# Last copies of a sequence on VectorE behind a subtraction, and a new order of the last units, in an attention and expert-routing kernel

## Chip, cores, metric

One core of a Trainium2 chip runs the whole program. The metric is device time of one execution in microseconds (us). The kernel before takes 702.86 us, the median of three runs (702.64 to 704.63).

## What is computed

Inputs are q, k, v of shape (8 sequences, 8 heads, 576 tokens, 64) and the weights of a mixture of 8 experts.

```
out_up    = repeat(softmax(0.125 q_d k_d^T) v_d, 4)        # q_d, k_d, v_d: means over groups of 4 tokens
out_local = softmax(where(|i-j| < 4, 0.125 q k^T, -1e9)) v
x         = (out_up + out_local) as 4608 tokens x 512
logits    = x @ w_gate                                     # 4608 x 8
# all (token, expert) pairs by falling logit; an expert takes 576 tokens at most
out[mask_e] = relu(x[mask_e] @ w1[e]) @ w2[e]
```

The order of the logits decides which expert a token goes to, so the logits of all tokens must stand before the first expert can be chosen.

## The kernel before, in words

The program has two stages. The attention stage (class Attention) makes x and the logits, the expert stage counts logits against thresholds, picks an expert, gathers its 576 tokens and runs its two products. This document is about the attention stage; the expert stage's code is untouched.

Attention works on 36 units of 128 tokens. A unit is four windows of 32 tokens of local attention: `loc_s` (s0, s1: local scores into PSUM, then row maximum L544 and subtraction L545 on VectorE, and an exponential L547 on ScalarE, called four pieces later), `loc_t` (t: transposes L555 of the exponentials, copied out of PSUM by ScalarE, L566), `loc_v` (v0, v1: product with v L577, and `norm`, three VectorE instructions L453, L454, L456 for each half), `log_a` (adds the up part, L587; on VectorE for units below 27 and for unit 35, on GpSimd for 27 to 34), `store` (x to DRAM on SyncE's queue), `log_t` (lt: four transposes of x L597 and a copy by ScalarE) and `log_m` (lm: the logits, copied to `lg` by VectorE). For a unit below UF = 33 the copy of lt is an fp16 high part (`hi`, L609, ScalarE) and an fp16 remainder (`lo`, L610, VectorE), and lm is eight short fp16 products (L625, L628). For units 33, 34 and 35 lt is one fp32 copy (L604, ScalarE) and lm is four fp32 products (L621).

Each of the 8 sequences b also needs: eight transposes of q and k (`trw`, L330), called here by letter, half and side: q00, k00, q01, k01, q10, k10, q11, k11; after each, two copies of 64x512 out of PSUM by `evac` (L310 to L316). One transpose of the 16 last groups (`trt`, L343) with two copies of 128x256. Sums over four tokens on GpSimd (`gsum`, L303, L306, called after k01 and k11, and `gsum_v` after k11). The down-sampled attention (`down_s`: scores, maximum L370, subtraction L372, exponentials L378; `down_t`: transposes L394, L399 and a copy each by `evac`; `down_v`: products and norm).

`evac` picks the engine of a copy: it counts calls (a pair counts once) and takes VectorE where the pattern EV has a 1. EV = (0, 0, 0, 0, 1) over 13 calls of a sequence moves from place to place. PSUM buffers called g are a ring of six (NG), shared by trw, trt, t, v0, v1, lt, lm and the down products: a product waits until the buffer six uses back has been read.

The order is written out: `run` gives every stage of every unit a due time, sorts by it, and emits the instructions in that order; each engine and each DMA queue executes its own in that order. The due time of a stage is u + LOC, and for LOC of 2 and more it is u + 2 + (LOC - 2) * (1 - 0.14 * max(u - 33, 0)) + max(0.72 - 0.55 u, 0). So v0 and v1 of unit 35 are due at 36.842 and 36.843, `add` (`log_a`) of units 32, 33 and 34 at 36.425, 37.425 and 38.085, lt of units 32 to 35 at 37.433, 38.433, 38.952 and 39.472, and lm of units 31 to 35 at 39.317, 40.317, 41.317, 41.433 and 41.548. `after(n, f)` puts a call n pieces (TensorE stages) later. `setup` (class Routing) turns logits into sort keys in steps; units 0 to 24 are done early (L725 to L728), its comparisons L834 at 38.45 and later, and units 25 to 35 right after the last logits.

Of the kernel before, what the change touches and what calls it, by code (L numbers as in the profile page):

```python
# [11 lines left out]
AF = mybir.ActivationFunctionType  # L12
OP = mybir.AluOpType
# [13 lines left out]
GM = 128  # L27
# [3 lines left out]
NT = NTOK // 128  # L31
E, F = 8, 1024
XS = 32.0
# [13 lines left out]
FH = 2  # L47
FL = 4
FT = 3
PEL = ("s0", "s1", "t", "v0", "v1", "lt", "lm")  # L50
TW = (0.23, 2.44)
DW = (0.15, 1.9)
# [9 lines left out]
XB = 6  # L62
NPT = 2
PEV = (0,0)
EV = (0, 0, 0, 0, 1)
UPB = 6
UPE = 1.5
VWE, VWU = 2.0, 33
CMP = (7, 38.1, 0.05)
ADDU = UPB * 9 // 2  # L70
DX = 0
SETUP = {24: 0, 35: 25}
SPACE = 0.365
GS = 32.0
# [8 lines left out]
E1 = 0.55  # L83
UE = 33
CE = 0.14
UF = 33
UL = 30
TX = 0.0
VX = 0.0
# [15 lines left out]
class Attention:  # L105
# [88 lines left out]
    def after(self, n, f, key=None):  # L194

        self.due.append((self.now + n, f, key))
# [112 lines left out]
    def evac(self, out, in_, more=False):  # L309

        self.nev += not more
        ev = EV if self.nev > EN0 else EV0
        if ev[self.nev % len(ev)]:
# [9 lines left out]
    def trw(self, b, which, hh, s):  # L323

        nc = self.nc
        src = self.nat[which, b]
        p = self.ps.tile([128, 2, GM, 2], F32, name="g", bufs=NG)
        for a in range(2):
            for fp in range(2):
                nc.tensor.transpose(p[:, a, :, fp], src[:, 4 * hh + 2 * a + s, 2 * fp:2 * fp + 2].rearrange("p f d -> p (f d)"),  # L330
                                    self.ident)
        t = self.dest(b, which)[64 * s:64 * s + 64, 2 * hh:2 * hh + 2]
        for par in range(2):
            self.evac(t[:, :, par:4 * GM:2], p[64 * par:64 * par + 64].rearrange("p a i f -> p a (i f)"), par)

    def trt(self, b):

# [230 lines left out]
    def loc_v(self, u, g):  # L568
        nc = self.nc
        if g == 0:  # L570
            self.x[u] = self.wk.tile([128, HD], F32, name="x", bufs=XB)
        x = self.x[u]
        o = self.ps.tile([128, 512], F32, name="g", bufs=NG)
        pt = self.ptw[u % NPT]
        for h in range(4):
            for i in range(2):
                nc.tensor.matmul(o[64 * i:64 * i + 64, 65 * h:65 * h + 65],  # L577
                                 pt[:, 2 * (h % 2) + i, 2 * g + h // 2].rearrange("p b q -> p (b q)"),
                                 self.vw[u % 4][:, i, 4 * g + h], start=True, stop=True)
        self.norm(o, x[:, 256 * g:256 * g + 256].rearrange("p (h d) -> p h d", h=4), 4, 1.0)  # L580
        if g and u == NT - 1:
            self.log_a(u)

    def log_a(self, u):
        nc = self.nc
        x = self.x[u]
        (nc.gpsimd if ADDU <= u < NT - 1 else nc.vector).tensor_tensor(x, x, self.up[u], op=OP.add)  # L587

    def store(self, u):
        getattr(self.nc, STQ).dma_start(self.x_dram[128 * u:128 * u + 128], self.x[u])  # L590
# [1 line left out]
    def log_t(self, u):  # L592
        nc = self.nc
        x = self.x[u]
        p = self.ps.tile([128, 4, 128], F32, name="g", bufs=NG)
        for c in range(4):
            nc.tensor.transpose(p[:, c], x[:, 128 * c:128 * c + 128], self.ident)  # L597
        pf = p.rearrange("p c t -> p (c t)")
        if u >= UF:
            if u < NT - 1:  # L600
                xt = self.wk.tile([128, HP, G], F32, name="kdt").rearrange("p h k -> p (h k)")[:, :512]
            else:
                xt = self.wk.tile([128, H, D], F32, name="xu", bufs=1).rearrange("p h d -> p (h d)")
            nc.scalar.activation(xt, pf, AF.Copy, scale=XS * GS)  # L604
            self.xt[u] = xt.rearrange("p (c t) -> p c t", c=4)
            return
        xt = self.wk.tile([128, 2, 4, 128], F16, name="xt", bufs=TB)
        hi = xt[:, 0].rearrange("p c t -> p (c t)")
        nc.scalar.activation(hi, pf, AF.Copy, scale=XS)  # L609
        self.after(FT if u < UE - 2 else 1, lambda: nc.vector.scalar_tensor_tensor(xt[:, 1].rearrange("p c t -> p (c t)"), pf, XS, hi,  # L610
                                                              op0=OP.mult, op1=OP.subtract), ("x", u))
        self.xt[u] = xt

    def log_m(self, u):
# [3 lines left out]
        l = self.ps.tile([128, 2, E], F32, name="g", bufs=NG)  # L618
        if u >= UF:
            for c in range(4):  # L620
# [12 lines left out]
    def transposes(self, b):  # L633
        out = []
        for hh in range(2):
            for s in range(2):
                for w in "qk":
                    def f(w=w, hh=hh, s=s):
                        self.trw(b, w, hh, s)
                        if b and s and w == "k":  # L640
                            self.gsum(b, "k", 2 * hh)
                            self.gsum(b, "q", 2 * hh)
                            if hh:
                                self.gsum_v(b)

                    out.append(f)

        return out[:2] + [lambda: self.trt(b)] + out[2:]
# [5 lines left out]
    def run(self, after, ready):  # L654
# [14 lines left out]
        for b in range(B):  # L669
            u0, up = 9 * b // 2, 9 * (b - 1) // 2  # L670
            t = self.transposes(b)
# [13 lines left out]
            if b + 1 < B:  # L685
                for i, (w, at) in enumerate(NEXT):
                    at = max(up + at + (SH1 if b == 1 else 0), -1.0) if b else LD1[i]
                    f = lambda b=b, w=w: self.load_nat(b + 1, w[0], int(w[1]) if w[1:] else None)
# [15 lines left out]
        work = [(at, 0, i, f, False) for i, (at, f) in enumerate(other)]  # L704
        work += [(at, 1, i, f, True) for i, (at, _, f) in enumerate(fill)]
        work += [(at, 1, 10 ** 6 + i, f, False) for i, (at, f) in enumerate(loads)]
        for u in range(NT):
            if u > 1:
                for c in range(4):
                    at = max(u - (VWT0 if u < UV else VWE if u >= VWU else VWT) + VWS * c, u - 3.999 + LOC["v0"])  # L710
                    f = lambda u=u, c=c: self.load_vw(u, (c,))
                    work.append((at, 0, 0, (lambda f=f: self.paced(f)) if at > PACE0 else f, False))
            for j, (name, lag) in enumerate(LOC.items()):
                at = u + lag
                if lag >= 2.0:

                    at = u + 2.0 + (lag - 2.0) * (1.0 - CE * max(u - UE, 0)) + max(E0 - u * E1, 0.0)
                if u >= UL:
                    at += {"t": TX, "v": VX, "v0": VX, "v1": VX}.get(name, 0.0)
                if name == "add" and u == NT - 1:  # L720
                    continue
                if name == "up":
                    at = max(at - (UPE if u >= NT - 2 else 0.0), end[(4 * u + 3) // NW])
                work.append((at, 2, j, stage[name](u), name in PEL))
                if name == "lm" and u in SETUP:  # L725
                    steps = after(SETUP[u], u + 1)
                    work += [(at + SPACE * k if u == NT - 1 or k < CMP[0] else CMP[1] + CMP[2] * k, 3, k,
                              lambda g=steps: next(g, None), False) for k in range(24)]  # L728
        work.sort(key=lambda z: z[:3])
        for *_, f, pe in work:  # L730
# [45 lines left out]
class Routing:  # L776
# [86 lines left out]
    def next(self, mm):  # L863
        if self.pad:
            self.behind_(mm, self.pad)
        return mm
# [637 lines left out]
```

## Time and profile before

| | us |
|---|---|
| median of three runs | 702.86 |
| the profiled execution, its own time | 703.13 |
| its span, first to last instruction | 701.5 |
| around the span | 1.63 |
| last logits of unit 35 copied (L622) at | 252.2 |
| TensorE / VectorE / ScalarE / GpSimd busy in the span | 648.6 / 521.7 / 337.7 / 245.9 |

Times in rows are microseconds from the start of the span. PE is TensorE's products, PEld its weight loads, DVE VectorE, ACT ScalarE, POOL GpSimd, SP SyncE. A row of the timeline gives start, length, engine, line, operation, output and inputs, count; in brackets is how long the engine sat idle before it and what ended that. Lengths of neighbours on one engine overlap a little; the step from start to start is the price.

### The profile page before, as it was taken

How to read it: one execution, taken by the hardware profiler on the slowest of the kernel's cores; microseconds unless marked ns; L12 is line 12 of the kernel's file. 1: busy time of each engine (PE TensorE's matmuls, PEld its weight loads, DVE VectorE, ACT ScalarE, POOL GpSimd, SP SyncE). 2: the span in 40 equal slices, each digit the busy share in tenths (PEclk: the TensorE clock that was granted, in tenths of full speed). 3: DMA queues.
4: the chain of work that ended last, by engine and by line, in shares of the span. 5: the costliest groups of instructions: out<-in, count | busy, mean ns of one | idle time of the engine just before them, and what ended most of it. 6: DMA issues, size and time to landing. Idle time of an engine off the chain costs nothing.

```text
span 701.5 us, 21944 instructions
## 1 busy us (share of the span) xinstructions
PE 648.6 (92%) x8938; PEld 451.3 (64%) x8938; DVE 521.7 (74%) x1544; ACT 337.7 (48%) x650; POOL 245.9 (35%) x320
## 2 busy tenths in 40 slices
PE   7789999899898957999999999999999999999994
PEld 4577777778787744764674575674674764755741
DVE  5697879878789887988887797897897876624500
ACT  4568778788686513523432443444334424424410
POOL 4886485665927412203303204104104115202011
PEclk9899999999999975999999999999999999999997
DMA  9967878868786614507308627548358169714001
GB/s 264 237 166 222 233 188 235 240 184 223 200 221 171 209 68 139 170 1 262 114 6 311 129 93 243 110 155 213 76 213 203 29 244 211 296 39 97 1 30 39
DMA packets 132157, 113.73 MB, mean 162 GB/s; under 512 B 81240, under 2 KB 109912, under 8 KB 132056
## 3 DMA queue, kind: packets, MB, share of 16 engines
q1 hardware_dynamic: 124760, 90.76, 45.7%
q0 software_dynamic: 6432, 20.98, 9.5%
q8 instruction: 71, 1.16, 0.7%
q10 hardware_dynamic: 864, 0.58, 0.3%
q14 instruction: 30, 0.25, 0.1%
HBM read 85.74 MB, written 19.46 MB: 150 GB/s over the span
## 4 chain that ended last, share of the span: by engine, by line
PE 50%; DVE 17%; issue 16%; ACT 7%; DMA 4%; POOL 4%; SPq 1%; ACTq 0%; POOLq 0%; DVEq 0%
PE pX L1332 16%; PE pH L1291 14%; PE g L577 2%; PE pR L886 2%; PE g L555 2%; DVE wl L1214 2%; PE s L535 2%; PE g L330 2%; POOL out_dram L1342 1%; PE g L597 1%; DMA nat<-in_k_dram 1%; PE pH L1198 1%; ACT kt L316 1%; POOL xg L1229 1%; ACT qt L316 1%
## 5 line engine op out<-in xcount | busy, mean ns | idle before, releaser
L1291 PE MATMUL pH<-xt,wh 128*128 128x256 f16 (+1 forms) x1024 | 191.2, 286 | 1.2 <-ACT xt L1250 0.5
L1332 PE MATMUL pX<-wh,ht 128*128 128x512 f16 (+1 forms) x640 | 178.0, 379 | 0.0
L1291 PE MATMUL pH<-xt,wl 128*128 128x320 f16 (+1 forms) x512 | 144.6, 286 | 0.0
L1332 PEld LDWEIGHTS <-ht 128*128 128x128 f16 (+1 forms) x960 | 82.7, 100 | 94.7 <-issue 4.7
L1332 PE MATMUL pX<-wl,ht 128*128 128x512 f16 (+1 forms) x320 | 117.6, 379 | 0.0
L1291 PEld LDWEIGHTS <-wh 128*128 128x128 f16 x1024 | 97.6, 98 | 29.6 <-issue 5.3
L1342 POOL DMA_INDIRECT out_dram<-y,idx x40 | 42.3, 1058 | 178.3 <-ACT y L1339 156.1
L1315 ACT ACTIVATE ht<-pH 128x512 f16<-128x512 f32 (+1 forms) x128 | 45.6, 407 | 114.4 <-PE pH L1291 114.4
L1214 DVE SCALAR_TENSOR_TENSOR wl<-nat,wh 128x512 f16<-128x512 f32 x128 | 83.5, 686 | 16.1 <-ACT wh L1212 13.7
L1339 ACT ACTIVATE y<-pX 128x512 f32<-128x512 f32 (+1 forms) x40 | 23.7, 594 | 101.4 <-PE pX L1332 58.9
L1318 DVE SCALAR_TENSOR_TENSOR ht<-pH,ht 128x512 f16<-128x512 f32 (+1 forms) x128 | 52.3, 449 | 26.1 <-ACT ht L1315 25.6
L1212 ACT ACTIVATE wh<-nat 128x1024 f16<-128x1024 f32 x64 | 67.3, 1053 | 3.8 <-DMA nat<-in_moe_w_dram 3.8
L1229 POOL DMA_INDIRECT xg<-x_dram,idx x40 | 43.1, 1079 | 61.6 <-DVE used L1112 33.4
L1291 PEld LDWEIGHTS <-wl 128*128 128x128 f16 x512 | 49.9, 98 | 12.7 <-issue 0.8
L566 ACT COPY pt<-g 64x512 f32<-64x512 f32 x72 | 41.8, 580 | 27.5 <-PE g L555 26.5
L577 PE MATMUL g<-vw,pt 128*64 128x65 f32 x1152 | 43.5, 225 | 4.0 <-issue 1.5
L577 PEld LDWEIGHTS g<-vw,pt 128*64 128x64 f32 x1152 | 37.8, 137 | 10.5 <-issue 5.0
L330 PE MATMUL g<-ident,nat 128*128 128x128 f32 x256 | 40.4, 283 | 4.2 <-DMA nat<-in_q_dram 3.7
L1031 POOL MEMSET f<- 128x1 bf16 x8 | 0.8, 106 | 118.3 <-DVE sumf L940 44.1
L1258 DVE SCALAR_TENSOR_TENSOR xs<-xg,xs 128x512 f16<-128x512 f32 (+1 forms) x30 | 20.4, 688 | 28.3 <-ACT xs L1257 28.1
L316 ACT COPY kt<-g 64x512 f32<-64x512 f32 (+1 forms) x60 | 38.3, 638 | 6.5 <-PE g L330 5.5
L303 POOL TENSOR_TENSOR gtmp<-kt 128x576 f32<-128x576 f32 x14 | 16.1, 1147 | 54.7 <-ACT kt L316 39.4
(229 smaller groups left out, 1155.5 us busy)
## 6 DMA issues: line engine op xcount, KB each, us to landing
nat<-in_moe_w_dram SPq DMA_DIRECT2D x28, 1024.0 KB
vw<-in_v_dram SPq DMA_DIRECT2D x136, 78.0 KB
x_dram<-x SPq DMA_DIRECT2D x36, 256.0 KB
nat<-in_q_dram SPq DMA_DIRECT2D x32, 256.0 KB
nat<-in_k_dram SPq DMA_DIRECT2D x32, 256.0 KB
nat<-in_v_dram SPq DMA_DIRECT2D x28, 256.0 KB
up<-up_dram SPq DMA_DIRECT2D x9, 256.0 KB
nat<-in_moe_w_dram SPq DMA_DIRECT2D x4, 512.0 KB
```

What stands on the lines that cost most here:

```text
L316: self.nc.scalar.copy(out, in_)
L330: nc.tensor.transpose(p[:, a, :, fp], src[:, 4 * hh + 2 * a + s, 2 * fp:2 * fp + 2].rearrange("p f d -> p (f d)"), self.ident)
L566: self.nc.scalar.copy(out, in_)
L577: nc.tensor.matmul(o[64 * i:64 * i + 64, 65 * h:65 * h + 65], pt[:, 2 * (h % 2) + i, 2 * g + h // 2].rearrange("p b q -> p (b q)"), self.v ...
L1212: nc.scalar.activation(hi, r, AF.Copy, scale=sc)
L1214: nc.vector.scalar_tensor_tensor(lo[:, a:a + LOP], r[:, a:a + LOP], sc, hi[:, a:a + LOP], op0=OP.mult, op1=OP.subtract)
L1229: self.fetched = nc.gpsimd.indirect_dma_start(out=xg[:n], out_offset=None, in_=self.x, in_offset=bass.IndirectOffsetOnAxis(ap=idx[:n, c:c ...
L1291: mm = nc.tensor.matmul(p[:, s, :s1 - s0], w[d][a][:, 128 * f:128 * f + 128], xt[:, b, d, s0:s1], start=j == 0, stop=j == len(seq) - 1)
L1315: last = nc.scalar.activation(hi, q, AF.Relu)
L1318: low = nc.vector.scalar_tensor_tensor(lo, q, 0.0, hi, op0=OP.max, op1=OP.subtract)
L1332: mm = nc.tensor.matmul(p[o:o + m], ht[:, f, h0:h0 + m], w[4 + f // 2][b][:, 512 * (f % 2):512 * (f % 2) + 512], start=j < parts, stop=j > ...
L1342: i = nc.gpsimd.indirect_dma_start(out=self.out, in_=y[:n], in_offset=None, out_offset=bass.IndirectOffsetOnAxis(ap=idx[:n, c:c + 1], axis=0))
```

## The change

In sequences 2 to 7 the two copies of k11 always go to VectorE, and they are emitted four pieces after the transpose with the sums that follow (`after(FK, ...)`), which is behind the subtraction L545 of the unit then running. These copies no longer count in `evac`, so a sequence has 12 counted calls, and the new EV, a pattern of six, hits the same two places each time: `trt` and k01. From sequence 2 on this gives:

- to VectorE: trt of 2, 3, 4, 6, 7, k01 of 2, 4, 5, 6, 7, k11 of 2, 3, 4, 6, 7 (k11 of 5 was there and moves behind the subtraction);
- to ScalarE: q11 of 2, q00, q01, k10 of 4, q10 of 6, k00 and q11 of 7, and five copies of transposed probabilities (`down_t`); in `down_t` of 7 the two last copies change places.

Among the last units: unit 33 takes the fp16 way (UF = 34); the remainder of unit 31 is put behind the norms of unit 35; the fp32 copies of lt are made in halves; the add of unit 35 is split, its first 256 columns on GpSimd in `loc_v` (due 36.842) and its second on VectorE (36.843); lt of 35 moves to 39.0, ahead of lm of 31, lm of 34 to 39.5, ahead of lm of 32 and 33, lm of 35 to 41.4; of the early comparisons the first moves to 35.34, the second to 39.1.

```diff
+FK = 4
-EV = (0, 0, 0, 0, 1)
+EV = (0, 1, 0, 0, 0, 0)
+ENDS = {("lt", 35): 39.0, ("lm", 34): 39.5, ("lm", 35): 41.4}
-CMP = (7, 38.1, 0.05)
+CMP = (7, 35.34, 39.1)
-UF = 33
+UF = 34
@@ trw
-        for par in range(2):
-            self.evac(t[:, :, par:4 * GM:2], p[64 * par:64 * par + 64].rearrange("p a i f -> p a (i f)"), par)
+        late = b > 1 and which == "k" and hh and s
+
+        def copies():
+            for par in range(2):
+                out, in_ = t[:, :, par:4 * GM:2], p[64 * par:64 * par + 64].rearrange("p a i f -> p a (i f)")
+                if late:
+                    nc.vector.tensor_copy(out, in_)
+                else:
+                    self.evac(out, in_, par)
+            if b and s and which == "k":
+                self.gsum(b, "k", 2 * hh)
+                self.gsum(b, "q", 2 * hh)
+                if hh:
+                    self.gsum_v(b)
+
+        if late:
+            self.after(FK, copies, ("e", b))
+        else:
+            copies()
@@ loc_v
-        if g and u == NT - 1:
-            self.log_a(u)
+        if u == NT - 1:
+            part = slice(256 * g, 256 * g + 256)
+            (nc.vector if g else nc.gpsimd).tensor_tensor(x[:, part], x[:, part], self.up[u][:, part], op=OP.add)
@@ log_a
-        (nc.gpsimd if ADDU <= u < NT - 1 else nc.vector).tensor_tensor(x, x, self.up[u], op=OP.add)
+        (nc.gpsimd if u >= ADDU else nc.vector).tensor_tensor(x, x, self.up[u], op=OP.add)
@@ log_t
-            nc.scalar.activation(xt, pf, AF.Copy, scale=XS * GS)
+            for c in range(2):
+                part = slice(256 * c, 256 * c + 256)
+                nc.scalar.activation(xt[:, part], pf[:, part], AF.Copy, scale=XS * GS)
...
-        self.after(FT if u < UE - 2 else 1, lambda: nc.vector.scalar_tensor_tensor(xt[:, 1].rearrange("p c t -> p (c t)"), pf, XS, hi,
+        self.after(FT if u < UE - 1 else 1, lambda: nc.vector.scalar_tensor_tensor(xt[:, 1].rearrange("p c t -> p (c t)"), pf, XS, hi,
@@ transposes
-                        if b and s and w == "k":
-                            self.gsum(b, "k", 2 * hh)
-                            self.gsum(b, "q", 2 * hh)
-                            if hh:
-                                self.gsum_v(b)
@@ run
+                at = ENDS.get((name, u), at)
...
-                    work += [(at + SPACE * k if u == NT - 1 or k < CMP[0] else CMP[1] + CMP[2] * k, 3, k,
+                    work += [(at + 0.2 + SPACE * k if u == NT - 1 else at + SPACE * k if k < CMP[0] else CMP[min(k - 6, 2)], 3, k,
```

## Rows read from the trace of the kernel before

**Rows 1.** Busy time by stretch: window, PE, PEld, DVE, ACT, POOL, clock, DMA, GB/s.
```profile
40.00:210.00 170.00, 158.16 (x4018) 131.76 (x4018) 141.21 (x396) 130.70 (x263) 108.13 (x149) 1.00 0.78 211
```

**Rows 2.** Timeline of PE: transposes L555 that waited for the exponential.
```profile
69.89 0.70 PE L555 MATMUL g<-ident,sw 128*128 128x128 f32 x4 [0.36 <-ACT sw L547]
...
97.82 0.66 PE L555 MATMUL g<-ident,sw 128*128 128x128 f32 x4 [1.05 <-ACT sw L547]
...
125.37 0.66 PE L555 MATMUL g<-ident,sw 128*128 128x128 f32 x4 [1.04 <-ACT sw L547]
...
214.29 0.66 PE L555 MATMUL g<-ident,sw 128*128 128x128 f32 x4 [0.90 <-ACT sw L547]
```

**Rows 3.** Timelines of DVE and ACT in sequence 4: the subtraction, the k11 copies.
```profile
122.04 0.48 DVE L545 TENSOR_TENSOR sw<-s,mx 128x304 f32<-128x304 f32 x1
...
123.08 1.27 ACT L316 COPY kt<-g 64x512 f32<-64x512 f32 x2
```

**Rows 4.** Timeline of DVE: its idle time behind the subtractions in sequences 3 and 4.
```profile
96.34 0.16 DVE L453 TENSOR_SCALAR den<-g 128x4 f32<-128x4 f32 x1 [0.71 <-PE g L577]
...
99.46 0.47 DVE L544 TENSOR_REDUCE mx<-s 128x8 f32<-128x304 f32 x1 [0.59 <-PE s L535]
...
123.90 0.16 DVE L453 TENSOR_SCALAR den<-g 128x4 f32<-128x4 f32 x1 [0.80 <-PE g L577]
...
127.12 0.47 DVE L544 TENSOR_REDUCE mx<-s 128x8 f32<-128x304 f32 x1 [0.69 <-PE s L535]
```

**Rows 5.** Timelines of ACT and DVE in sequence 2: a high part, and the q11 copies.
```profile
61.81 0.60 ACT L609 ACTIVATE xt<-g 128x512 f16<-128x512 f32 x1
...
62.71 1.40 DVE L314 COPY qt<-g 64x512 f32<-64x512 f32 x2
```

**Rows 6.** Timelines of DVE, ACT and PE in sequence 6: unit 25's maximum, subtraction, exponential, transposes.
```profile
185.38 0.47 DVE L544 TENSOR_REDUCE mx<-s 128x8 f32<-128x304 f32 x1 [0.34 <-PE s L535]
...
185.89 0.47 DVE L545 TENSOR_TENSOR sw<-s,mx 128x304 f32<-128x304 f32 x1
...
186.57 0.45 ACT L547 ACTIVATE sw<-sw 128x304 f32<-128x304 f32 x1
...
187.08 0.66 PE L555 MATMUL g<-ident,sw 128*128 128x128 f32 x4
```

**Rows 7.** Timeline of DVE: its first idle time after 211.2 in sequence 7.
```profile
220.37 0.47 DVE L544 TENSOR_REDUCE mx<-s 128x8 f32<-128x304 f32 x1 [0.22 <-PE s L535]
```

**Rows 8.** Timelines of PE and ACT: two waits of down-sampled attention, a trt copy.
```profile
51.73 0.55 PE L394 MATMUL g<-ident,sd 128*128 128x128 f32 x3 [0.33 <-ACT sd L378]
...
166.97 0.63 ACT L316 COPY qt<-g 128x256 f32<-128x256 f32 x1
...
168.86 0.55 PE L394 MATMUL g<-ident,sd 128*128 128x128 f32 x3 [0.75 <-ACT sd L378]
```

**Rows 9.** Timeline of PE in the last units.
```profile
244.96 1.22 PE L577 MATMUL g<-vw,pt 128*64 128x65 f32 x32 [0.65 <-DMA up<-up_dram]
...
248.60 0.66 PE L597 MATMUL g<-ident,x 128*128 128x128 f32 x4 [0.34 <-DVE lg L630]
...
249.31 1.93 PE L621 MATMUL g<-wgf,kdt 128*128 128x8 f32 x16
251.10 1.04 PE L621 MATMUL g<-wgf,xu 128*128 128x8 f32 x8
```

**Rows 10.** Timelines of POOL and DVE in the last units.
```profile
244.47 2.50 POOL L587 TENSOR_TENSOR x<-x,up 128x512 f32<-128x512 f32 x2 [0.66 <-PE g L597]
...
245.56 0.69 DVE L610 SCALAR_TENSOR_TENSOR xt<-g,xt 128x512 f16<-128x512 f32 x1 [0.69 <-ACT xt L609]
...
246.57 0.42 DVE L456 TENSOR_TENSOR x<-g,den 128x256 f32<-128x256 f32 x1
```

**Rows 11.** Instructions of L276 and L436: duration ns min/median/max, first and last start.
```profile
L276 POOL TENSOR_TENSOR vd<-gtv x16: 723/727/735, 24.6 to 221.2; 128x256 f32<-128x256 f32 x16
...
L436 DVE TENSOR_TENSOR own<-den,identb x8: 149/200/681, 42.5 to 233.2; 128x2 f32<-128x2 f32 x8
```

## The prediction

> **What bounds the kernel now.** The edits lie in the attention stage, whose last act is the copy of unit 35's logits; the expert stage starts from it and its code stays, so what moves that copy moves the end by as much. I read first the busy times by stretch, then TensorE's timeline for its idle times, then the other engines around each moved instruction. From 40 to 210 us TensorE is busy 158 of 170 us, VectorE 141, ScalarE 131 and GpSimd 108 [rows 1]: nothing has much room, and a microsecond taken from one engine helps only if TensorE or VectorE then waits less. TensorE's waits that the edits can reach are those of the transposes t for an exponential: 0.36, 1.05, 1.04 and 0.90 us [rows 2], 3.35 in all. Their cause is seen in sequence 4: the subtraction is done by 122.52, but ScalarE first makes the k11 copies, 123.08 to 124.35, then a high part and only then the exponential [rows 3], and t runs at 125.37. In the last units the end is made by TensorE: lt of unit 35 at 248.60, the fp32 logits of 33 and 34 (1.93, or 0.97 a unit), then unit 35's (1.04), done at 252.14 [rows 9].
>
> **The late pairs, sequence by sequence.** A pair of copies takes 1.40 us on VectorE and 1.27 on ScalarE [rows 3, 5]. On VectorE it now stands between the subtraction and the add and norms of the same unit, so these come 1.40 later except where VectorE stood idle.
>
> Sequence 3: VectorE's idle behind the subtraction is 0.71 and 0.59, nearly the pair [rows 4]; shortly after, q00 of sequence 4 leaves it (1.40 less). TensorE's 1.05 is won: -1.05.
>
> Sequence 4: room 0.80 + 0.69 = 1.49 [rows 4] against 1.40. TensorE can win 1.04, VectorE only 0.09. Each end has its row, TensorE's wait and VectorE's room; both engines are as busy there, so I take the middle, -0.55; the ends are -1.04 and -0.09.
>
> Sequence 2: a swap, q11 to ScalarE and k11 to VectorE. ScalarE's high part at 61.81 [rows 5] now stands behind q11 and is done 1.27 later, at 63.6. VectorE, free at 62.7 where it made q11 before [rows 5], needs that high part for its remainder and idles 0.9; the late pair then takes what q11 gave back. I take +0.87 (ends 0 and 1.27).
>
> Sequence 5: the pair was on VectorE already and goes from before the maximum to behind the subtraction: 0, with ends -0.1 and +0.6 (the idle time that it no longer fills).
>
> Sequence 6: the first idle time behind the subtraction of unit 24 that waits for TensorE's next scores is 0.34 [rows 6]. Of 1.40 some 1.06 stays: the subtraction that ended at 186.36 ends at 187.42, its exponential starts there instead of at 186.57 and ends at 187.87, and the transposes wait from 187.08 to then [rows 6]: +0.8 (ends 0 and 1.06).
>
> Sequence 7: q11 leaves VectorE and k11 comes. TensorE's wait of 0.90 goes, but VectorE's first idle time in that run is at 220.37 (0.22) [rows 7], and with equal work on it the next exponential comes no sooner: 0 (ends -0.9 and +0.2). What is late next there is VectorE itself.
>
> **The new pattern of copies.** The trt copies leave ScalarE, where they stand ahead of a down-sampled exponential (166.97, then the wait of 0.75 at 168.86; likewise 0.33 at 51.73) [rows 8]. I take both as won, -1.08: VectorE's own trt pair lies there ahead of norms with idle time behind. The k01 pairs, the copies of probabilities and the other exchanges I cost at nothing: the cover is ScalarE's and VectorE's idle time around down_v. If it is gone, each pair costs up to 1.40 less the idle time there. The sums on GpSimd start behind the late pair, but their products come several us later, so that is free too. On SyncE's queue nothing is moved.
>
> Sum of the stretch to 244: -1.05 - 0.55 + 0.87 + 0.8 - 1.08 = **-1.01 us**.
>
> **The last units.** Removed: 0.69 us of remainder (unit 31) ahead of the norms of 35 [rows 10], half of the last add, and 0.97 of fp32 logits (unit 33) against some 0.2 of fp16. Added: a remainder for 33, which hides before lm of 33. The first early comparison fits an idle gap of VectorE before the norms of unit 34, the second comes while it waits for the last logits: both 0.
>
> What counts is GpSimd's queue. By the due times its new half add (36.842) stands ahead of the adds of units 33 (37.425) and 34 (38.085), and waits for unit 35's first norm. That norm cannot start before the first half of v0 and v1, 244.96 + 0.61 = 245.57 [rows 9], and takes 0.82 (246.17, the end of the remainder, to 246.57 + 0.42) [rows 10]: 246.4. A GpSimd add of 256 columns takes 0.73 [rows 11], so add 33 starts at 247.1 and, with 1.25 each [rows 10], add 34 ends at 249.6. Before, these two ran from 244.47 to 246.97 [rows 10]. TensorE's lt of 33, of 34 and, behind them in its own queue, of 35 wait: lt of 34 at 249.65, lt of 35 some 0.6 later at 250.25 instead of 248.60 [rows 9]. From there: lt and one fp16 lm 0.71 (248.60 to 249.31), lm of 34 0.97, lm of 32 and 33 some 0.2 each, lm of 35 1.04 [rows 9]: 253.4 against 252.14, **+1.2 us**. The halved copies of 34 and 35 are not last: their bounds, 0.3 and 0.63 a half (half of 0.60 in rows 5; a 256-column copy in rows 8), move this by 0.2 at most. The ends of this term are -0.9 (the queue does not hold) and +1.6.
>
> VectorE's half add reads two operands from SBUF while GpSimd adds there. An instruction of that kind, L436, with two columns, took from 149 to 681 ns [rows 11], so something can hold it. The Trainium skill, SBUF — State Buffer, section Who interferes with whom, has this as an exclusive lock: a VectorE instruction with two SBUF inputs and a GpSimd instruction that reads SBUF run one after the other. By it the half add would either wait out add 33, which changes nothing since lt of 34 comes later still, or hold GpSimd up by some 0.35, and this term would be +1.2 to +1.6. The sum keeps 1.2.
>
> **Sum.** -1.01 + 1.2 = +0.2 against the profiled execution's 703.13, that is 703.3. That execution lies 0.27 above the median of 702.86, so I forecast **703.1**. A measurement of this kernel tells 0.3%, or 2.1 us, from no change: below 700.75 is faster, above 704.97 slower.
>
> **Rivals.**
> *All waits won.* If VectorE's delays are taken up by later idle time (it is idle 29 of 170 us [rows 1]), TensorE wins all of 3.35 + 1.08 and sequences 2 and 6 cost nothing: -4.4 + 1.2 gives 699.7 against the median. For it: TensorE is the busiest. Against it: the run without a gap in sequence 7. Chance 0.13.
> *The queue does not hold.* If adds 33 and 34 run before the half add, lt of 35 follows lt of 34 at 248.1, and 0.71 + 0.97 + 0.4 + 1.04 end at 251.2: -0.9, with -1.01 gives 700.9, and with the other waits of sequences 4 and 7 won as well 699.5. Only an order unlike the due times would do it. Chance 0.10.
> *VectorE decides (slower).* The added copies are five trt pairs and three more pairs, less five single copies: some 6 us more on VectorE. If every late pair costs like sequence 6 (0.8 in 3, 4, 6 and 7, 0.87 in 2) and no wait is won, that is +4.1 + 1.2: 708.2. It decides from the point at which the norm behind the pair starts later than the wait won on ScalarE; sequence 6 is past it, 3 is not. Chance 0.11.
> *It does not do what it says:* PSUM's ring could bring the late copies' wait back, since their buffer stays taken longer and t is six uses behind. In sequence 4 the pair would end some 1.4 behind the subtraction, at 123.9, ahead of the 125.37 at which t ran [rows 2, 3], so it does not; included in the rest, 0.06.
>
> **Numbers.** My forecast's case has 0.60, with a range of its own from 700.9 to 705.0 by the ends above. Faster: 0.13, half of 0.10, and 0.03 from the rest, 0.21. Slower: 0.11, 0.03 from the rest and 0.02 from the upper edge of my case, 0.16. Same: 0.63. The range runs from 699.5 to 705.0 and leaves out most of the slower rival and the outermost part of the fastest.
>
> **What would show it.** Right: the copies kt at the late places on VectorE behind L545; no wait above 0.3 us of L555 at sequences 3 and 4; a new wait near 0.8 us of L555 for unit 25; GpSimd's order of a 256-column L587, then two of 512, the last ending about 3.2 us behind v0 of unit 35; lt of 35 waiting for it; the last L622 1.2 us later behind the start of v0 of 35 than before (7.2). Wrong: adds 33 and 34 ahead of the half add, VectorE idle above 20% in 60 to 210, or a time below 700.7 or above 705.

## The result, and the profile after

The changed kernel takes **709.25 us** (median of 22 runs, 703.20 to 712.34) against 704.78 for the kernel before on the same chips (22 runs, 701.98 to 709.80): a ratio of **1.0058, 95% interval 1.0041 to 1.0074**, some 4.1 us slower (0.0058 x 704.78). The forecast was no change, 703.1 with a range from 699.5 to 705.0. The profiled execution takes 709.95; its span is 708.3 (before 701.5). Lines of the changed kernel have moved by up to 22: L545 is L564, L555 is L574, L577 is L596, L597 is L617, L621 and L622 are L643 and L644, L587 is L607. L602 is the half add, L341 a late copy.

**The last units.** Timelines of TensorE, VectorE and GpSimd of the changed kernel, to be read beside [rows 9, 10] (the 250.48 row is lt of unit 33, the 251.71 row lt of 34 and 35):

```profile
246.45 1.22 PE L596 MATMUL g<-vw,pt 128*64 128x65 f32 x32 [0.65 <-ACT pt L585]
...
250.48 0.66 PE L617 MATMUL g<-ident,x 128*128 128x128 f32 x4 [1.84 <-POOL x L607]
251.71 1.93 PE L617 MATMUL g<-ident,x 128*128 128x128 f32 x8 [0.57 <-POOL x L607]
...
253.68 1.85 PE L643 MATMUL g<-wgf,kdt 128*128 128x8 f32 x8
...
255.82 1.85 PE L643 MATMUL g<-wgf,xu 128*128 128x8 f32 x8
...
248.85 0.45 DVE L602 TENSOR_TENSOR x<-x,up 128x256 f32<-128x256 f32 x1
...
257.71 0.17 DVE L644 COPY lg<-g 128x8 f32<-128x8 f32 x1 [1.54 <-PE g L643]
...
248.30 0.73 POOL L602 TENSOR_TENSOR x<-x,up 128x256 f32<-128x256 f32 x1 [2.82 <-PE g L650]
248.98 2.67 POOL L607 TENSOR_TENSOR x<-x,up 128x512 f32<-128x512 f32 x2
```

GpSimd stood idle for 2.82 us in front of the half add of unit 35 while the adds of units 33 and 34 were queued behind it; they end at 251.65, and TensorE waits 1.84 and 0.57 us for them. The last logits are copied 257.71 - 246.45 = 11.26 us behind the start of v0 of unit 35; before it was 252.18 - 244.96 = 7.22. That is +4.0, nearly the whole loss. But the waits make only part of it: the fp32 logits of a unit, 1.04 in [rows 9], take 1.85. The granted clock tells why (windows; the last three columns are clock, DMA share, GB/s):

```profile
248.00:250.00 2.00, 0.64 (x12) 0.53 (x10) 1.90 (x8) 0.60 (x1) 1.70 (x2) 1.00 0.04 15
250.00:252.00 2.00, 0.95 (x6) 0.72 (x7) 0.86 (x3) 0.60 (x1) 2.00 (x4) 0.95 0.34 130
252.00:254.00 2.00, 2.00 (x18) 1.94 (x16) 0.93 (x3) 0.99 (x4) 0.24 (x2) 0.50 0.70 263
254.00:256.00 2.00, 2.00 (x25) 2.00 (x25) 0.38 (x4) 0.33 (x2) 0.00 (x0) 0.50 0.03 8
```

TensorE was busy 0.64 and 0.95 of two times 2 us, then its clock fell from 2.4 to 1.2 GHz, and everything behind the wait ran at half speed. In the kernel before it falls too, but only behind the logits, which are done at 252.18 (windows of before):

```profile
252.00:254.00 2.00, 0.59 (x14) 0.41 (x13) 1.65 (x10) 0.58 (x2) 0.27 (x4) 1.00 0.19 40
254.00:256.00 2.00, 0.50 (x7) 0.27 (x7) 1.43 (x7) 0.00 (x0) 0.00 (x0) 0.51 0.19 64
```

**The copies.** Sequences 2 to 7 (timelines of TensorE, VectorE and GpSimd, beside [rows 2, 5, 6, 8]):

```profile
70.75 1.03 PE L574 MATMUL g<-ident,sw 128*128 128x128 f32 x4 [1.79 <-ACT sw L566]
...
98.85 0.66 PE L574 MATMUL g<-ident,sw 128*128 128x128 f32 x4
...
125.19 0.66 PE L574 MATMUL g<-ident,sw 128*128 128x128 f32 x4
...
158.62 0.63 PE L617 MATMUL g<-ident,x 128*128 128x128 f32 x4 [0.49 <-DVE x L475]
...
170.34 0.63 PE L574 MATMUL g<-ident,sw 128*128 128x128 f32 x4 [0.28 <-DVE den L472]
...
188.50 0.66 PE L574 MATMUL g<-ident,sw 128*128 128x128 f32 x4 [0.28 <-ACT sw L566]
...
227.47 0.66 PE L617 MATMUL g<-ident,x 128*128 128x128 f32 x4 [0.85 <-POOL x L607]
...
63.45 0.69 DVE L632 SCALAR_TENSOR_TENSOR xt<-g,xt 128x512 f16<-128x512 f32 x1 [1.31 <-ACT xt L631]
...
65.66 1.39 DVE L341 COPY kt<-g 64x512 f32<-64x512 f32 x2
...
69.17 0.46 DVE L563 TENSOR_REDUCE mx<-s 128x8 f32<-128x304 f32 x1
...
214.97 1.15 POOL L305 TENSOR_TENSOR gtmp<-kt 128x576 f32<-128x576 f32 x1 [5.81 <-DVE kt L341]
```

The waits of 1.05 and 1.04 us in sequences 3 and 4 are gone. In sequence 2, VectorE waits 1.31 us for the high part that now stands behind q11; the pair follows, then norms and a remainder without a gap, and the next maximum comes late. TensorE waits 1.79 us for its exponential, and the transposes that follow take 1.03 us instead of 0.66: there too the clock has fallen (windows):

```profile
66.00:70.00 4.00, 2.96 (x113) 2.40 (x111) 3.78 (x11) 1.76 (x3) 2.71 (x3) 1.00 0.65 185
70.00:74.00 4.00, 3.25 (x81) 2.02 (x82) 3.79 (x12) 1.62 (x3) 3.69 (x8) 0.61 0.41 104
```

Between units 20 and 24 the wait of 0.75 us for the down-sampled exponential [rows 8] is gone too, but TensorE now waits 0.49 and 0.28 us for VectorE's norms, which stand behind the late pair of sequence 5 and behind a trt pair. In sequence 7, GpSimd's sums wait for the late pair (214.97); adds of the up part stand behind them in its queue, and at 227.47 lt waits 0.85 us for one of these adds.

VectorE is busy 146.1 of the 170 us of [rows 1], 5 more than before; ScalarE 124.2, 6 less.

### The profile page after: what moved, and what is told of

It is laid out like the page before. It is cut to its first block, busy times and chain, and to the rows that moved or that the text cites. A ratio compares the mean times of both kernels' runs of the same rounds, so it can differ in the third digit from the quotient of the medians.

```text
span 708.3 us, 21954 instructions
## 1 busy us (share of the span) xinstructions
PE 653.6 (92%) x8938; PEld 453.8 (64%) x8938; DVE 527.0 (74%) x1556; ACT 330.7 (47%) x641; POOL 246.4 (35%) x321
## 4 chain that ended last, share of the span: by engine, by line
PE 28%; issue 17%; DVE 11%; POOL 4%; ACT 2%; DMA 2%; another core or an unknown queue 0%; POOLq 0%; ACTq 0%; DVEq 0%
PE pH L1309 12%; PE pX L1350 11%; PE pR L904 2%; POOL out_dram L1360 2%; DVE wl L1232 2%; POOL xg L1247 2%; DVE ht L1336 1%; DMA xg<-x_dram,idx 1%; ACT wh L1230 1%; PE pH L1216 1%; DVE level L852 1%; DVE cmp L852 1%; ACT ht L1333 1%; DVE less L914 0%
## 5 line engine op out<-in xcount | busy, mean ns | idle before, releaser
L1360 POOL DMA_INDIRECT out_dram<-y,idx x40 | 42.1, 1053 | 179.8 <-ACT y L1357 154.6
L596 PE MATMUL g<-vw,pt 128*64 128x65 f32 x1152 | 43.3, 225 | 4.3 <-ACT pt L585 2.8
L596 PEld LDWEIGHTS g<-vw,pt 128*64 128x64 f32 x1152 | 37.9, 138 | 10.9 <-issue 4.9
L318 ACT COPY qt<-g 64x512 f32<-64x512 f32 (+1 forms) x49 | 30.7, 627 | 7.7 <-PE g L332 4.1
```

What stands on the lines that cost most here:

```text
L318: self.nc.scalar.copy(out, in_)
L1360: i = nc.gpsimd.indirect_dma_start(out=self.out, in_=y[:n], in_offset=None, out_offset=bass.IndirectOffsetOnAxis(ap=idx[:n, c:c + 1], axis=0))
```

## Experiments

Two theories stood at the start. A: the last units cost it, by GpSimd's queue and the clock that falls in the wait. B: VectorE decides, so the late pairs and the new pattern cost it. The measure for the last units is one distance in each profile, from the start of v0 of unit 35 to the last copy of logits ("tail" below: 7.22 before, 11.26 changed). A loss in us beside a ratio is the ratio less one times the median of before; a difference between two kernels is that of their ratios, times the same median.

**One part alone, and the other.** The last units' edits without those of the copies, and the copies' edits without those of the last units:

```diff
-EV = (0, 1, 0, 0, 0, 0)
+EV = (0, 0, 0, 0, 1)
-        late = b > 1 and which == "k" and hh and s
+        late = False
```

> The changed kernel without its edits to the copies: the old pattern, and the k11 pairs in their old place; only the new order of the last units is left. Theory A: about 4 us above the kernel before (1.005 to 1.007), with the last copy of logits some 11 us behind v0 of unit 35. Rival B: at most 1.2 us above the kernel before.

Measured: 709.27 us, ratio 1.0061 (1.0035 to 1.0088), +4.3 us, as A expected.

> The kernel before with the edits to the copies alone: the late k11 pairs and the new pattern, the last units as before. Theory A: between 1 us below and 1 us above the kernel before (my sum of the stretch was -1.0; the first units' maxima of the changed kernel's trace stood +1.1). Rival B: 3 us or more above the kernel before.

Measured: 706.11 us, ratio 1.0023 (1.0001 to 1.0044), +1.6 us, between A's 1 and B's 3. So both parts lose: the last units nearly all, as A has it, and the copies something between nothing and 3 us, where the forecast had a gain of 1.0. The profile of the last units alone does not show the tail of some 11 us that A expected:

```profile
249.18 0.66 PE L617 MATMUL g<-ident,x 128*128 128x128 f32 x4 [1.84 <-POOL x L607]
...
251.60 1.06 PE L643 MATMUL g<-wgf,kdt 128*128 128x8 f32 x8
```

The wait is the same 1.84, but the clock stays at 1.00 until the logits are out and the tail is 8.84. That execution took 705.51, the second shortest of the kernel's twelve (median 709.27). So the clock need not fall behind this wait although the instructions of the last units are the same; that it does fall in most executions is only inferred from their times.

**The wait and the clock told apart.** TensorE kept busy while it waits, by products into an unused buffer:

```diff
+        if u in (NT - 3, NT - 2):
+            q = self.ps.tile([128, 2, 512], F32, name="s", bufs=1)[:, 0]
+            for _ in range(8 if u == NT - 3 else 3):
+                nc.tensor.matmul(q, self.wm, self.wm[:, None].to_broadcast([128, 4, 128]), start=True, stop=True)
```

> The changed kernel with TensorE kept busy while it waits for GpSimd: eight products of 512 columns into an unused PSUM buffer ahead of lt of unit 33, and three ahead of lt of unit 34. The wait itself stays. Theory A with the clock as the larger part (1.2 us of wait, 2.8 us of half clock): lt of 33 still starts about 4.0 us behind v0 of unit 35, but the granted clock is 1.00 from 248 to 256 us, the fp32 logits take about 1.0 us a unit instead of 1.85, the last copy of logits comes 8.3 to 8.8 us behind v0 of 35 instead of 11.26, and the time is 2.5 to 3 us below the changed kernel. Theory A with the wait as the whole (the clock only follows): no gain, 0 to +0.5 us. Rival B: no statement beyond the tail, the distance to the kernel before stays at 3 us or more whatever the tail does.

Timeline of it, TensorE and then VectorE:

```profile
250.25 1.89 PE L618 MATMUL s<-wm 128*128 128x512 bf16 x8
252.24 0.66 PE L621 MATMUL g<-ident,x 128*128 128x128 f32 x4
252.73 0.81 PE L618 MATMUL s<-wm 128*128 128x512 bf16 x3
...
254.65 1.06 PE L647 MATMUL g<-wgf,kdt 128*128 128x8 f32 x8
255.97 1.04 PE L647 MATMUL g<-wgf,xu 128*128 128x8 f32 x8
...
257.04 0.17 DVE L648 COPY lg<-g 128x8 f32<-128x8 f32 x1 [0.72 <-PE g L647]
```

lt of 33 starts 252.24 - 248.20 = 4.04 behind v0 of 35, as in the changed kernel (4.03), so the wait for GpSimd is unchanged; but the logits take 1.06 and 1.04, and the tail is 8.84. By the profiles the wait, less what the unit of fp32 logits that is gone gives back, is 8.84 - 7.22 = 1.6 us and the half clock 11.26 - 8.84 = 2.4. The times do not show it: 707.59 us, ratio 1.0048 (1.0022 to 1.0074), 0.7 us below the changed kernel by the ratios instead of 2.5 to 3, which is within the noise of both.

**The one edit that does it.** The kernel before with nothing but the split add:

```diff
-        if g and u == NT - 1:
-            self.log_a(u)
+        if u == NT - 1:
+            part = slice(256 * g, 256 * g + 256)
+            (nc.vector if g else nc.gpsimd).tensor_tensor(x[:, part], x[:, part], self.up[u][:, part], op=OP.add)
```

> The kernel before with one edit: the add of unit 35 in two halves, the first on GpSimd, at its due time ahead of the adds of units 33 and 34. Theory A: lt of 33 waits for GpSimd about 2 us, and the last copy of logits comes 9 to 12 us behind v0 of unit 35 instead of 7.22, by whether the clock falls in the wait; 2 to 4.5 us above the kernel before. If the other edits of the last units carry the loss: within 1 us of the kernel before.

Measured: 712.13 us, ratio **1.0096** (1.0066 to 1.0126), +6.8 us, more than the whole change. Timelines and windows:

```profile
253.23 1.11 PE L598 MATMUL g<-ident,x 128*128 128x128 f32 x4 [2.24 <-POOL x L588]
...
257.28 3.56 PE L622 MATMUL g<-wgf,kdt 128*128 128x8 f32 x16
...
262.59 0.17 DVE L623 COPY lg<-g 128x8 f32<-128x8 f32 x1 [1.54 <-PE g L622]
...
251.05 0.72 POOL L583 TENSOR_TENSOR x<-x,up 128x256 f32<-128x256 f32 x1 [3.52 <-PE g L629]
251.74 3.18 POOL L588 TENSOR_TENSOR x<-x,up 128x512 f32<-128x512 f32 x2
```

```profile
251.00:253.00 2.00, 0.00 (x0) 0.00 (x0) 1.93 (x7) 0.50 (x1) 1.95 (x2) 0.99 0.00 0
253.00:255.00 2.00, 1.14 (x5) 0.75 (x5) 2.00 (x2) 0.56 (x1) 2.00 (x3) 0.50 0.34 131
```

TensorE does nothing from 251 to 253 and then runs at half clock; three units of fp32 logits stand behind it here, two in the changed kernel. The tail is 262.59 - 248.80 = 13.79. The same kernel with TensorE kept busy in the wait, by the same lines as above:

> The kernel before with the half add on GpSimd, as in the run of it alone, and TensorE kept busy in the wait by eight products of 512 columns ahead of lt of unit 33 and three ahead of lt of unit 34. If the fall of TensorE's clock is the larger part of that edit's loss: the clock stays 1.00 to the last logits, which are copied 9.0 to 9.6 us behind v0 of 35 instead of 12.08, and the time is 2.5 to 4 us below the run of the half add alone. If the wait is the whole loss and the clock only follows it: no gain, within 1 us of it.

Measured: 706.45 us, ratio 1.0064 (1.0039 to 1.0088): 0.0032, or 2.3 us, below the half add alone. Its fp32 logits (timeline):

```profile
252.03 1.93 PE L626 MATMUL g<-wgf,kdt 128*128 128x8 f32 x16
253.82 1.32 PE L626 MATMUL g<-wgf,xu 128*128 128x8 f32 x8
```

1.93 instead of 3.56; the clock falls only in the last 1.32. The tail is 255.18 - 244.49 = 10.69, 3.1 below 13.79. (The 12.08 of the expectation goes to the copy before the last; to that copy it is 254.00 - 244.49 = 9.51 here, within the 9.0 to 9.6 expected.) lt of 33 starts 4.44 behind v0 of 35, 4.43 without the products, so the wait is the same. Both pairs of profiles show the clock as a loss of its own, 2.4 and 3.1 us, with the wait as the rest. The times point the same way, 0.7 and 2.3 us, but in both pairs the intervals overlap, so the split between wait and clock rests on the profiles.

**Taking GpSimd's wait away, two ways.** First, both halves on VectorE:

```diff
-            (nc.vector if g else nc.gpsimd).tensor_tensor(x[:, part], x[:, part], self.up[u][:, part], op=OP.add)
+            nc.vector.tensor_tensor(x[:, part], x[:, part], self.up[u][:, part], op=OP.add)
```

> The changed kernel with one edit: the first half of the add of unit 35 runs on VectorE too, so GpSimd's queue holds only the adds of units 33 and 34. Theory A (the last units cost it: TensorE waits for GpSimd's adds behind the half add, and its granted clock falls in that wait): the last copy of logits comes 7 to 7.5 us behind the start of v0 of unit 35 instead of 11.26, the granted clock stays 1.00 until then, and the time is about 4 us below the changed kernel, within 1.5 us of the kernel before. Rival B (VectorE decides: the late pairs and the new pattern cost 3 us or more in the stretch to 244 us): the last units give back 1.2 us at most, and it stays 3 us or more above the kernel before.

Measured: 707.35 us, ratio 1.0041 (1.0015 to 1.0067), 2.9 us above the kernel before, where A had 1.5 at most and B 3 or more; tail 8.85, not 7 to 7.5. Timelines of TensorE, VectorE and GpSimd:

```profile
246.96 0.63 PE L617 MATMUL g<-ident,x 128*128 128x128 f32 x4 [1.39 <-DVE x L475]
...
249.92 1.78 PE L643 MATMUL g<-wgf,xu 128*128 128x8 f32 x8
...
244.55 1.52 DVE L602 TENSOR_TENSOR x<-x,up 128x256 f32<-128x256 f32 x1
...
246.85 0.42 DVE L602 TENSOR_TENSOR x<-x,up 128x256 f32<-128x256 f32 x1
...
243.29 2.50 POOL L607 TENSOR_TENSOR x<-x,up 128x512 f32<-128x512 f32 x2 [1.18 <-DMA up<-up_dram]
```

A half add takes 1.52 us beside GpSimd's adds, which end at 245.79, and 0.42 behind them. Held there, it holds the second norm of unit 35; lt of unit 34 waits 1.39 for that norm (by the profile; the norm empties a PSUM buffer), and the clock falls in the last logits. One wait took the place of another.

Second, the half add left on GpSimd but behind the adds of 33 and 34:

```diff
-                    continue
+                    at = 38.09
```

with `log_a` of unit 35 adding the first 256 columns on GpSimd and `loc_v` the second on VectorE.

> The changed kernel with the half add of unit 35 still on GpSimd, but emitted behind the adds of units 33 and 34. Theory A (GpSimd's queue, and the clock that falls in the wait, make the last units dear): GpSimd ends the adds of 33 and 34 about 2.9 us behind the start of v0 of unit 35 instead of 5.2, lt of 33 waits less than 0.5 us for it, the clock stays 1.00 up to the last logits, which are copied 6.5 to 7.5 us behind v0 of 35, and the time is 3 to 4 us below the changed kernel. Rival C (VectorE's half add of two SBUF inputs is held while GpSimd adds, as the 1.52 us of it in the kernel with both halves on VectorE): it takes over 1 us, lt of 35 waits for it, and the last copy comes 8 us or more behind v0 of 35.

```profile
248.76 0.66 PE L617 MATMUL g<-ident,x 128*128 128x128 f32 x4 [0.52 <-POOL x L607]
249.74 0.63 PE L617 MATMUL g<-ident,x 128*128 128x128 f32 x4 [0.32 <-DVE lg L652]
...
250.40 1.04 PE L643 MATMUL g<-wgf,kdt 128*128 128x8 f32 x8
251.70 1.04 PE L643 MATMUL g<-wgf,xu 128*128 128x8 f32 x8
...
247.96 1.02 DVE L601 TENSOR_TENSOR x<-x,up 128x256 f32<-128x256 f32 x1
...
246.20 3.37 POOL L607 TENSOR_TENSOR x<-x,up 128x512 f32<-128x512 f32 x3 [1.67 <-DMA up<-up_dram]
```

Measured: **705.58 us**, ratio 1.0020 (0.9992 to 1.0049), 2.7 us below the changed kernel by the ratios, a little less than the 3 to 4 expected; tail 252.77 - 245.56 = 7.21, clock 1.00 until then. VectorE's half is held again (1.02 us), as rival C had it, but the tail stays below C's 8. It is no shorter than before although one unit of fp32 logits is gone: lt of 35 starts 4.18 us behind v0 of 35, before 3.64. GpSimd's half ends just ahead of it (249.57), and the copy of logits (L652) that it waits for by the profile stands behind the held add in VectorE's queue; which of the two decides was not told apart. With the copies as before:

> The new order of the last units with the half add of unit 35 behind the adds of units 33 and 34, and the copies as before. Theory A: 0.9 us below to 0.4 us above the kernel before, 4 us below the last units as changed. Rival C (VectorE's half add is held by GpSimd's adds): 1.5 to 2 us above the kernel before.

```profile
254.00 1.85 PE L643 MATMUL g<-wgf,xu 128*128 128x8 f32 x8
...
250.06 1.12 DVE L601 TENSOR_TENSOR x<-x,up 128x256 f32<-128x256 f32 x1
```

Measured: 704.01 us, ratio 0.9985 (0.9958 to 1.0013), 5.4 us below the last units as changed (1.0061), and here the intervals do not overlap: the order of three adds is the loss of the last units. The profiled execution took 706.00; in it the clock falls in the last logits (1.85), and the tail is 255.89 - 247.66 = 8.23.

**Which of the copies.** Sequence 2 with its last two pairs as before:

```diff
-        late = b > 1 and which == "k" and hh and s
+        late = b > 2 and which == "k" and hh and s
+        own = b == 2 and hh and s
...
+                elif own and which == "q":
+                    self.nev += not par
+                    nc.vector.tensor_copy(out, in_)
+                elif own:
+                    nc.scalar.copy(out, in_)
```

> The copies alone (the kernel before with the late pairs and the new pattern), with sequence 2 left as before in its last two pairs: q11 on VectorE, k11 on ScalarE. Theory A2 (sequence 2's late pair is what the copies cost: its 1.4 us stand bare on VectorE, TensorE waits 1.8 us for the next exponential, and its clock falls from there to about 74 us): the wait of 1.8 us at 70 us is gone, the clock is 1.00 in 60 to 80 us, and the time is 1.5 to 2.5 us below the kernel with all late pairs, so 0 to 1 us below the kernel before. Rival B2 (every late pair costs alike): 0.3 us below the kernel with all late pairs, still 1 us above the kernel before.

Measured: 705.06 us, ratio 0.9991 (0.9967 to 1.0015); the wait at 70 us is gone and the clock is 1.00 there. That favours A2, though the intervals of this kernel and of all late pairs (1.0001 to 1.0044) still overlap. The unit maxima (L544, L563) in all profiles say more: time from one to another, medians with the extremes, over six kernels with the copies as before and five with all of them changed. A maximum runs on VectorE, whose own order the change moves; so the column "TensorE" gives the difference again between the starts of the same units' scores (first products into s), which TensorE runs in an order that the change does not touch.

| units | sequence | as before | changed | difference | TensorE | forecast |
|---|---|---|---|---|---|---|
| 0 to 5 | trt of 2 | 40.78 (40.15 to 41.07) | 40.97 (40.86 to 41.95) | +0.2 | -0.5 | -0.33 |
| 5 to 10 | 2 | 30.99 (30.81 to 31.63) | 32.40 (31.14 to 32.49) | +1.4 | +2.1 | +0.87 |
| 10 to 15 | 3 | 35.18 (34.96 to 36.20) | 33.92 (33.91 to 34.79) | -1.3 | -1.3 | -1.05 |
| 15 to 20 | 4 | 31.88 (31.31 to 32.25) | 31.22 (30.34 to 32.63) | -0.7 | -0.4 | -0.55 |
| 20 to 24 | 5, an exponential | 27.72 (26.98 to 28.91) | 28.59 (27.70 to 28.79) | +0.9 | -0.2 | -0.75 |
| 24 to 27 | 6 | 13.68 (13.13 to 16.46) | 14.09 (13.71 to 14.45) | +0.4 | +0.9 | +0.8 |
| 27 to 35 | 7, last units | 46.39 (45.72 to 47.04) | 46.76 (46.30 to 47.41) | +0.4 | +0.4 | 0 |
| 0 to 35 | all | 226.52 (226.04 to 230.11) | 227.42 (225.06 to 230.16) | +0.9 | +0.9 | -1.01 |

The total is the same by both, its parts are not. Sequence 2 splits in two: by the maxima 31.14 and 31.16 in the two profiles whose clock stays 1.00 between 60 and 80 us, 32.40 to 32.49 in the three where it falls; by TensorE's starts 31.24 and 31.26 against 32.48 to 32.54, and 30.35 (30.17 to 30.99) with the copies as before. So the fall costs 1.2 to 1.3 us; at full clock the pair costs 0.9 by TensorE's starts, as forecast, and next to nothing by the maxima. In two of the five kernels, and in both with all pairs but that of 2, the clock falls once more, between 179.8 and 187.2 us (here in the run with the busy wait, a window):

```profile
184.00:188.00 4.00, 4.00 (x117) 3.68 (x117) 3.79 (x11) 1.88 (x4) 2.11 (x3) 0.60 0.26 82
```

There TensorE stood idle 2.0 to 2.8 us in the scores of unit 24, and the profile names no engine that it waited for. No kernel with the copies as before shows this fall. Sequence 3 and 4 are won as forecast, so they were tried alone, on the old pattern EV:

```diff
-        late = b > 1 and which == "k" and hh and s
+        late = b in (3, 4) and which == "k" and hh and s
+        self.nev += bool(late)
+        own = b == 4 and which == "q" and not hh and not s
...
+                elif own:
+                    self.nev += not par
+                    nc.scalar.copy(out, in_)
```

> The kernel before with late pairs in sequences 3 and 4 alone, and q00 of 4 on ScalarE; every other copy and the last units as before. By the steps between unit maxima in the traces so far (medians with and without the change: unit 10 to 15 -1.6 us, unit 15 to 20 -0.5): 1.5 to 2 us below the kernel before, if the gain of these two sequences lasts to the end. If the loads or VectorE take it back before the last units: within 0.7 us of the kernel before, with the maximum of unit 20 early and that of unit 35 not.

Measured: 702.87 us, ratio 0.9972 (0.9939 to 1.0006): 2.0 us faster by the ratio, as expected in size, but not clear of no change. In its profile the clock falls in the last logits (timeline):

```profile
251.18 1.66 PE L644 MATMUL g<-wgf,xu 128*128 128x8 f32 x8
```

**The rest of the change.** The last units with the add of 35 whole on VectorE, as it was; and both with late pairs of 3 and 4, and with all late pairs but that of 2:

```diff
-        if u == NT - 1:
-            part = slice(256 * g, 256 * g + 256)
-            (nc.vector if g else nc.gpsimd).tensor_tensor(x[:, part], x[:, part], self.up[u][:, part], op=OP.add)
+        if g and u == NT - 1:
+            self.log_a(u)
...
-        (nc.gpsimd if u >= ADDU else nc.vector).tensor_tensor(x, x, self.up[u], op=OP.add)
+        (nc.gpsimd if ADDU <= u < NT - 1 else nc.vector).tensor_tensor(x, x, self.up[u], op=OP.add)
```

> The new order of the last units without the split add: the add of unit 35 whole on VectorE behind its norms, as before; the copies as before. If the half add on GpSimd is the whole fault of the last units, GpSimd ends the adds of 33 and 34 about 2.9 us behind the start of v0 of unit 35, lt of 35 starts 3.7 us behind it as before, and one unit less of fp32 logits shows: the last copy 6.5 to 6.9 us behind v0 of 35 instead of 7.22, 0.3 to 0.7 us below the kernel before. If the other edits (lt of 35 early, the moved remainder, the comparisons) cost too: 7.5 us or more behind v0, 0.5 us or more above the kernel before.

Measured: 703.69 us, ratio 0.9982 (0.9957 to 1.0007), 1.3 us below the kernel before but not clear of no change; tail 7.33, with the clock falling in the last logits (1.55 instead of 1.04; without that 6.8, as expected).

> Both together: late pairs in sequences 3 and 4 with q00 of 4 on ScalarE, and the new order of the last units with the add of unit 35 whole on VectorE. If both parts hold and add up: 2 to 2.5 us below the kernel before. If the gain of 3 and 4 is lost on the way: 0.3 to 0.7 us below it.

Measured: 702.96 us, ratio 0.9976 (0.9951 to 1.0001), 1.7 us below, between the two expectations and not clear of no change. Its tail, 252.12 - 245.25 = 6.87, is as forecast for the other edits of the last units.

> The changed kernel with two parts taken out: the split add (whole on VectorE, as before) and the late pair of sequence 2 (q11 on VectorE, k11 on ScalarE, as before). If these two carry the whole loss: 4 to 6 us below the changed kernel and 0 to 1 us below the kernel before. If late pairs of 5, 6 and 7 cost as well: 1 us or more above the kernel before.

Measured: 703.56 us, ratio 0.9993 (0.9967 to 1.0019), 4.6 us below the changed kernel, with no overlap of the intervals; tail 6.93. Without the split add and the late pair of sequence 2 the rest of the change is worth nothing that these runs can measure. No version is shown to beat the kernel before; the likeliest is the late pairs of 3 and 4, with or without the last units' other edits.

## Why the prediction was wrong

**The last units** (+1.2): this step failed, by its size. Its mechanism is as forecast: the half add ahead in GpSimd's queue, lt of 33, 34 and 35 behind it. The queue's part was 0.4 short: 8.84 - 7.22 = 1.6, the upper end given for it, since the half add started later than reckoned and the two adds behind it took 2.67 instead of 2.50, so add 34 ended 5.2 behind v0 of 35 where the working had 249.6 - 244.96 = 4.6 (the 3.2 in its last paragraph was a slip). What was missing is that every product behind the wait was priced with a row taken at full clock: 0.97 and 1.04 of [rows 9]. They took 1.85 in the profiled execution, and the tail grew by 4.0 instead of 1.2; the last units alone lost 4.3 us by their times. The prediction looked at the clock in one row [rows 1] and never asked what a TensorE idle for 1.84 us would do to it.

**VectorE's half add beside GpSimd** was costed at nothing or 0.35. In the changed kernel that holds: 0.45 us, as it started ahead of GpSimd's add of unit 33 (248.85 against 248.98), and the two adds took 0.17 longer. Where GpSimd's add is ahead, it took 1.52, 1.12 and 1.02.

**The stretch to 244** (-1.01): measured +0.9 in the profiles, +1.6 (0.1 to 3.1) by the copies alone. By TensorE's starts, sequences 3, 4 and 6 are within 0.3 of their terms (for sequence 6, two of the five profiles hold a fall of the clock). Three terms failed. Sequence 2 was +0.87 and is +2.1: the price at full clock is right, 0.9, and the fall of the clock, again not asked for, adds 1.2. Of the exponentials' -1.08 the 0.33 came (units 0 to 5), but not the 0.75: that wait is gone, while TensorE waits 0.45 to 1.08 us there for VectorE, which by the working had idle time to spare behind the trt pair. And GpSimd's sums behind the late pair, free in the working because their products come later, were not free in sequence 7: what came late were the adds behind them in the queue, for which lt waits 0.67 to 0.85 us in four of the five profiles, and in none with the copies as before. The rest of the 0.4 between units 27 and 35 stays open.

**The rivals.** The time came out near that of "VectorE decides" (708.2), for another reason: the late pairs do not cost alike (3 and 4 win, 2 and 6 lose), and with sequence 2 left out the rest shows no loss (0.9991, 0.9967 to 1.0015). The queue held, and PSUM's ring did not bring back the waits of sequences 3 and 4.

**The signs named.** Right: the late copies' place, no wait at sequences 3 and 4, GpSimd's order, lt waiting for it. Wrong: the wait for unit 25, 0.28 instead of 0.8 (TensorE was itself late by 0.92 us in the scores before it; two other kernels with the same copies show 0.67 and 0.94), and the last copy, 4.0 us later behind v0 instead of 1.2. Of the signs of being wrong one came, a time above 705; adds 33 and 34 stayed behind the half add, and VectorE was idle 14% from 60 to 210 us.

## What to carry to other kernels

An in-order engine's queue is part of the price of an instruction put on it: ask what stands behind it and who waits for that; moving one add behind two others won 2.7 us in the changed kernel and 5.4 in the last units alone. Where a change gives TensorE a new wait, price what follows at both clocks, and keep waits out of the last stage, where nothing behind takes the loss up. And read a stage's gain from several profiles, by the same two landmarks, on the engine that ends the stage: single profiles with the same copies differ by 4 to 5 us from unit 0 to 35, and a landmark on VectorE gave sequences 2 and 5 other prices than one on TensorE.

## What the hardware showed

**The clock.** In all fifteen profiles TensorE's clock falls from 2.4 to 1.2 GHz in the last units, 4.2 to 10.7 us behind the start of v0 of unit 35; what differs is whether the last logits are out by then. In the kernel before they are out 1.9 us ahead of the fall, in the last units alone 1.0 ahead; in the changed kernel the fall comes 5.9 us ahead of them, right behind the waits of 1.84 and 0.57. In sequence 2 it fell behind a wait of 1.79 or 1.80 us in three of five profiles, so the same wait does not decide it alone. In the kernel with the late pairs of 3 and 4, whose waits ahead are 0.17 and 0.16 us, it fell in the last logits all the same (1.66 instead of 1.04). A fall cost 1.2 to 1.3 us in sequence 2; in the last units 2.4 to 3.1 where it came right behind the wait, and 0.3 to 0.8 where it came only in the last logits.

**VectorE and GpSimd.** A VectorE add of two SBUF operands, 0.42 to 0.45 us alone, took 1.02 to 1.52 when it came behind the start of one of GpSimd's adds of two SBUF operands, and ended 0.28 or 0.29 us behind the second of these; in the kernel with the add alone, two comparisons on VectorE took 2.42 us (0.75 is one elsewhere), and GpSimd's two adds 3.18 instead of 2.50. The Trainium skill, SBUF — State Buffer, section Who interferes with whom, calls this an exclusive lock and says that the order of issue, not the operation, decides who waits; the 0.45 and the 1.52 us of one add agree.
